# Laying attention output in token order on chip, and storing 128 tokens as one transfer

## The chip, the cores and the metric

The kernel runs on one NeuronCore of one Trainium2 chip. The time is the device time of one execution in microseconds; of several executions the median is given. Five engines work side by side, each through its own list of instructions in order: TensorE (PE), VectorE (DVE), ScalarE (ACT), GpSimd (POOL) and SyncE (SP). PE's loads of stationary weights are shown as PEld. A transfer (DMA) is issued by one of the queues of SP, ACT or POOL, and 16 DMA engines carry it out.

## The reference

Eight batches of attention with twelve heads whose scores are mixed across heads before the softmax and after it, then a two-layer network with a squared relu on each token:

```python
scores = scale * np.matmul(q, k.transpose(0, 1, 3, 2))   # q, k, v: 8 x 12 x 448 x 64
scores = np.einsum('bhij,hg->bgij', scores, w_pre)
attn = np.exp(scores - np.max(scores, axis=-1, keepdims=True))
attn = attn / (np.sum(attn, axis=-1, keepdims=True) + 1e-09)
attn = np.einsum('bhij,hg->bgij', attn, w_post)
x = np.matmul(attn, v)           # to (8 * 448) x (12 * 64) = 3584 x 768
h = np.maximum(x @ w_in, 0.0)    # w_in 768 x 2048
out = h * h @ w_out              # w_out 2048 x 768, out 3584 x 768, float32
```

## The kernel before

**Tokens and chunks.** The 448 tokens of a batch fall into a tail of the last 64 (block r = 0) and three blocks r = 1, 2, 3 of 128: a block holds every third of the first 384 tokens, so that row p of block r is token 3p + r - 1. Scores are made per block (`score`, L718): matmuls into a PSUM bank, copied as bf16 to `snat`, 128 tokens by 12 heads by 448 keys. To mix heads, the kernel needs head and token together in the partitions. `relayout` (L769) does that with one DMA on SP's queue for each chunk of ten tokens (`sch`, 120 rows of ten tokens by twelve heads). 45 such chunks make a batch, 360 the whole kernel.

**Which ten tokens.** In blocks 1 to 3 a relayout takes every twelfth row of the block: o, o + 12, and so on (L798). From batch 1 on (`PAIR_FROM`) two chunks are mixed together (`mix_two`, L824), in quarters of the PE array, and the ten tokens of a result are every sixth row of one half of 120. Rows 120 to 127 of the blocks are gathered in chunks of their own (cc = 0). In batch 0, block 1 and the first chunk of block 2 are "direct" (`is_direct`): they are mixed without a relayout, and their ten tokens stand side by side.

**A chunk** (`chunk`, L850): PE mixes the heads into a bank (L891, L837); VectorE takes the maximum of each row (L902); ScalarE computes the exponential with its sum (L905); VectorE takes reciprocals (L912); GpSimd multiplies the second mixing matrix by them (`wq`, L915); PE mixes heads again and turns the result over at once, four matmuls into a bank of 112 keys by 4 x 12 x 10 (L922); VectorE or ScalarE copies the bank to `atb` as bf16 (`f_ac`, L929, through the helper `copy`, L533 on VectorE and L535 on ScalarE). `places` (L808) says at which columns of `atb` the tokens of the chunk stand: ten next to one another, chunk after chunk. So a column of `atb` is a position and not a token.

**The rest.** `av` (L956) multiplies `atb` with the values (L968) and copies to `xt`; its list of chunks that it needs comes from `touches` (L980). `unit` (L1010) runs the network over 128 or 256 positions: first layer L1027, relu L1041 or L1045, square on GpSimd L1048, second layer L1066, and copies of 128 positions by 384 columns into one of two buffers `osb`. When both halves are there, the stores go out (L1090). Because positions are not tokens, `pieces` (L1101) gives two transfers for 128 positions of a block: 120 rows, whose destination steps through chunks and slots, and 8 rows for the chunks of their own. The 64 positions of a tail are one transfer. Both go through GpSimd's queue, except for the last 128 positions, which go out in three column cuts, the 120 rows on SP's queue and the 8 rows on ACT's.

**Order.** The program's order is written by a planner (class `Planner`, L147 for `run`) before the kernel is built. Every piece of work is an operation with engines that may take it, an assumed duration and a priority; the planner plays time forward and lists, for each engine, what comes next. A copy that VectorE or ScalarE may do goes to whichever comes free first. A chunk's number n is its priority; scores and relayouts of a chunk have n minus `AHEAD` and so come earlier (L737, L777, L797). Network matmuls have a priority behind all chunks and fill what is left of PE. Transfers are modelled with two queues (`moved`, L142): a number of rows, and ns for each row alone and beside the other queue.

The copy and the stores:

```python
for half, x0, s0, w in where:
    copy(
        eng, atb[half][:, :, :, x0:x0 + w].rearrange("p j g m -> p (j g) m"),
        slots[ak][0:P_KEYS, 0:NB * H * ns].rearrange("p (a m) -> p a m", m=ns)[:, :, s0:s0 + w],
    )
```

Of the kernel before, what the change touches and what calls it, by code (L numbers as in the profile page):

```python
# [23 lines left out]
NJ = 3  # L24
# [16 lines left out]
PIECE = NPAIR // 2  # L41
NE = 6
NSCH = 14
AHEAD = 7.7
FIFO = 50
IDLE_NS, IDLE_COLS, IDLE_FROM, IDLE_END, IDLE_LOW = 112, 256, 1300, 130000, 0.62
SPELL, PHASE, DROP, RISE = 3413, 1700, 0.4, 0.8
# [292 lines left out]
def kernel(  # L340
# [370 lines left out]
    def is_direct(b, c):  # L711
        return b == 0 and C0[1] <= c <= C0[2]
# [95 lines left out]
    def places(b, c):  # L808
        r, cc = block_of(c)
        rest, first = (0, NS) if b % 2 else (P_ROWS, 0)  # L810
        if r == 0:
            return [(0, rest + CI * cc, 0, CI)]
        half, base = [(0, first), (1, 0), (1, P_ROWS)][r - 1]
        if cc > 0:
            return [(half, base + CI * (cc - 1), 0, CI)]
        if b == 0 and r > 1:
            return [(0, rest + 62, 0, 2), (1, 120, 2, 8)] if r == 2 else [(1, P_ROWS + 120, 0, 8)]
        return [
            [(0, rest + 60, 0, 2), (0, first + 120, 2, 8)],
            [(0, rest + 62, 0, 2), (1, 120, 2, 6)],  # L820
            [(1, 126, 0, 2), (1, P_ROWS + 120, 2, 8)],
        ][r - 1]

    def mix_two(b, cs):  # L824
# [25 lines left out]
    def chunk(b, c):  # L850
# [76 lines left out]
                )  # L927

        def f_ac(eng):  # L929
            for half, x0, s0, w in where:  # L930
                copy(
                    eng, atb[half][:, :, :, x0:x0 + w].rearrange("p j g m -> p (j g) m"),
                    slots[ak][0:P_KEYS, 0:NB * H * ns].rearrange("p (a m) -> p a m", m=ns)[:, :, s0:s0 + w],
                )

# [20 lines left out]
    def av(b, half, gs, x0, x1):  # L956
        to = [(max(c0, x0), t0 + max(x0 - c0, 0), min(c0 + w, x1) - max(c0, x0)) for c0, t0, w in spans(b % 2, half)]
        to = [span for span in to if span[2] > 0]
        keys = [("g", "v", b, half, g, x0) for g in gs]

        def mms(*got):
            for g, slot in zip(gs, got):
                v_ = slot[:, :].rearrange("p (a c) -> p a c", a=2)
                for i in range(2):
                    c2 = 2 * g + i
                    for jb in range(NB):
                        for hh in range(2):
                            nc.tensor.matmul(  # L968
                                v_[64 * hh:64 * hh + 64, i, 0:x1 - x0],
                                lhsT=vs[:, 2 * c2 + hh, jb, :],  # L970
                                rhs=atb[half][:, jb, 2 * c2 + hh, x0:x1],
                                start=(jb == 0), stop=(jb == NB - 1),
                            )

        def evac(eng, g, key):
            v_ = slots[key][:, :].rearrange("p (a c) -> p a c", a=2)
            for c0, t0, w in to:
                copy(eng, xt[:, 2 * g:2 * g + 2, t0:t0 + w], v_[:, :, c0 - x0:c0 - x0 + w])

        def touches(c):  # L980
            return any(h_ == half and p0 < x1 and p0 + w > x0 for h_, p0, _, w in places(b, c))

        cs = [place_of(b, c) for c in range(NCHUNK) if touches(c)]
        old = []
        if b == 1:
            old += relay_of[0]
        if b >= 2:
            for a, z in units_of(b // 2 - 1):
                if any(a < t0 + w and z > t0 for _, t0, w in to):
                    old += h_op[b // 2 - 1, a]  # L990
        pri = max(cs) + 3
        mm = add(
            "PE", 60 + 48 * (x1 - x0) // 14 * len(gs), pri, keep(keys, mms), [ac_op[n] for n in cs] + v_in[b] + old, lat=200,
            bank=keys, mode=COLS,
        )
        av_op.setdefault((b, half), []).append(mm)
        for g, key in zip(gs, keys):
            xc = add(
                {"ACT": 440, "DVE": 540} if len(to) == 1 else {"ACT": 650, "DVE": 750}, 0, pri,
                lambda eng, g=g, key=key: evac(eng, g, key), [mm], lat=100, frees=key,  # L1000
            )
            for _, t0, w in to:
                xc_op.setdefault(b // 2, []).append((t0, t0 + w, xc))
# [6 lines left out]
    def unit(pair, ui):  # L1010
# [47 lines left out]
        for mt in range(w // 128):  # L1058
            whole = not (z == W2B and mt == 1 and pair == B // 2 - 1)
            cuts = [0, 384, DMODEL] if whole else [0, 384, 640, DMODEL]  # L1060
            for nt, (c0, c1) in enumerate(zip(cuts, cuts[1:])):
                key = ("f", ix, "o", mt, nt)
                for f0 in range(0, FT, OSTEP):
                    def mms(slot, f0=f0, mt=mt, c0=c0, c1=c1):
                        for ft in range(f0, f0 + OSTEP):
                            nc.tensor.matmul(  # L1066
                                slot[:, 0:c1 - c0], lhsT=h2_[:, ft, mt * 128:(mt + 1) * 128],
                                rhs=w2[:, ft, c0:c1],
                                start=(ft == 0), stop=(ft == FT - 1),
                            )  # L1070
                    if f0 == 0:
                        prev = add("PE", (12 + (c1 - c0) * 5 // 3) * OSTEP / 4, fill + 20 + 4 * mt + 2 * nt, keep(key, mms),
                                   [prev] + sq_op[ix][0:max(1, OSTEP // nf)] + w2_in[0:1 if ix < SOON else 4], lat=0, bank=key)
                    else:
                        prev = add("PE", (12 + (c1 - c0) * 5 // 3) * OSTEP / 4, FILL, lambda key=key, mms=mms: mms(slots[key]), [prev, w2_in[f0 // 4]] + sq_op[ix][0:(f0 + OSTEP + nf - 1) // nf], lat=0)
                    o_op[ix].append(prev)
                end = add("WAIT%s" % str(key), 0, 0, lambda: None, [prev], lat=200)
                si = ix_store[0]

                def evac(eng, key=key, si=si, c0=c0, c1=c1):  # L1080
                    copy(eng, osb[si % 2][:, c0:c1], slots[key][:, 0:c1 - c0])

                ev = add({"DVE": 80 + (c1 - c0) * 25 // 24, "ACT": 165 + (c1 - c0) * 5 // 7}, 0, 0, evac, [end, st_op.get(si - 2)] + ([m_op[n_] for n_ in direct] if si < 2 else []), lat=100, frees=key)
                evs = evs + [ev] if nt == 1 and whole else [ev]
                if nt == 1 or not whole:
                    done = []
                    for rows, dst, o in pieces(pair, a + mt * 128, None if whole else (c0, c1)):
                        side_ = not whole and rows <= CI
                        def store(dst=dst, o=o, rows=rows, si=si, e0=0 if whole else c0, e1=DMODEL if whole else c1, eng=nc.scalar if side_ else nc.gpsimd if whole else nc.sync):
                            eng.dma_start(out=dst, in_=osb[si % 2][o:o + rows, e0:e1])  # L1090
                        done.append(add("ACT" if side_ else "POOL" if whole else "SP", 510 if rows <= CI else 830 if whole else 930, FILL, store, evs))
                    for op in done:
                        op.store = whole
                    st_op[si] = pl.moved("LOAD" if whole else "DMA", 64, 31, 31, 0, done, 700)
            if whole:
                ix_store[0] += 1

# [3 lines left out]
    def pieces(pair, pos, part=None):  # L1101
        e0, e1 = (0, DMODEL) if part is None else part
        got = []
        for bb in range(2):
            row = (2 * pair + bb) * S
            for j, first in enumerate(PLACES[bb]):
                o = first + bb * S - pos
                if not 0 <= o < 128:
                    continue
                if j == NJ:  # L1110
                    got.append((NS, out[row + TAIL:row + S, e0:e1], o))
                    continue
                if row == 0 and j == 0:
                    got.append((P, out[0:TAIL, :].rearrange("(p r) e -> p r e", r=NJ)[:, 0, e0:e1], o))
                    continue
                view = out[row:row + CPR * CI * NJ, :].rearrange(
                    "(s c r) e -> r c s e", c=CPR // 2 if 2 * pair + bb >= PAIR_FROM else CPR, r=NJ,
                )
                got.append((CPR * CI, view[j, :, :, e0:e1], o))
                part_ = out[row:row + TAIL, :].rearrange("(p r) e -> p r e", r=NJ)  # L1120
                got.append((8, part_[CPR * CI:P, j, e0:e1], o + CPR * CI))
        return got

    def gate(step):
# [209 lines left out]
```

## Time and profile before

| | |
|---|---|
| median of 3 executions | 573.57 us (572.86 to 578.93) |
| the profiled execution | 574.74 us, span 573.0 us |
| mean granted PE clock | 0.996 of full speed |
| PE / VectorE / ScalarE / GpSimd busy | 560.2 / 495.3 / 451.5 / 378.3 us |
| store issues on GpSimd's queue | 53: 22 of 120 rows, 22 of 8 rows, 8 of 64 rows, 1 of 128 rows |
| atb copies of 112 x 480 | 178 on VectorE, mean 648 ns; 158 on ScalarE, mean 562 ns |
| HBM read, written | 45.61 MB, 11.01 MB |

The span runs from the first to the last instruction of the profiled execution; some 1.7 us lie around it. A line of a group reads: line of the kernel, engine, operation, what is written from what, partitions x elements and type, count, then busy time in us and the mean ns of one, then the time the engine sat idle just before these instructions and what ended it. Lines of the helper `copy` carry L533 or L535 whatever is copied, so the tile's name tells them apart. A "busy" PE need not run at its peak: the time from one matmul's end to the next one's says how fast it goes.

### The profile page before, as it was taken

Reading aid. Unit: us, or ns where it says so; the run is one execution under the profiler, and the core shown is the slowest. Engines: PE = TensorE matmul, PEld = TensorE weight load, DVE = VectorE, ACT = ScalarE, POOL = GpSimd, SP = SyncE. Lnnn points to the kernel's source line nnn. Section 1 sums busy time; section 2 is a strip of 40 time slices with the busy share of each in tenths; the row PEclk is TensorE's granted clock in tenths of the full one; section 3 lists DMA queues with packets and bytes.
Section 4 is the critical chain, followed back from the end, with each engine's and each line's share of the span. In section 5 each row is a group of like instructions: output and inputs, shape, how many; then the busy total and the mean of one; then the engine's idle time right before and its main releaser. Section 6 shows DMA issues by size and latency. Waiting matters only on the chain.

```text
span 573.0 us, 17975 instructions
## 1 busy us (share of the span) xinstructions
PE 560.2 (98%) x6323; PEld 396.6 (69%) x6323; DVE 495.3 (86%) x1101; ACT 451.5 (79%) x1194; POOL 378.3 (66%) x697
## 2 busy tenths in 40 slices
PE   8999999999999899999999999999999999999996
PEld 4767756785676657677677577767667566767784
DVE  7999999999999689998897998988799888988441
ACT  6799999789888688888988888987988888887200
POOL 9867447784795539767687468957598454747451
PEclk9999999999999989999999999999999999999999
DMA  9999849963999529954798649975496745422011
GB/s 134 212 201 220 160 108 213 179 161 97 178 185 143 142 81 180 182 147 103 142 208 139 148 112 162 178 141 142 108 204 153 154 125 100 131 78 79 5 53 56
DMA packets 132505, 80.89 MB, mean 141 GB/s; under 512 B 61748, under 2 KB 129062, under 8 KB 132414
## 3 DMA queue, kind: packets, MB, share of 16 engines
q0 software_dynamic: 51664, 33.45, 37.4%
q1 hardware_dynamic: 80702, 46.26, 34.2%
q8 instruction: 49, 0.80, 0.5%
q14 instruction: 42, 0.34, 0.2%
q10 hardware_dynamic: 48, 0.02, 0.0%
HBM read 45.61 MB, written 11.01 MB: 99 GB/s over the span
## 4 chain that ended last, share of the span: by engine, by line
PE 89%; DVE 5%; DMA 2%; ACT 2%; issue 1%; POOL 1%; DVEq 0%; POOLq 0%; ACTq 0%
PE bank L1066 26%; PE bank L1027 25%; PE bank L922 14%; PE bank L732 7%; PE bank L968 7%; PE bank L837 5%; PE bank L891 3%; DVE mn L902 2%; DMA sch<-snat 1%; ACT es L905 1%; PE bank L897 1%; DVE osb L880 1%; DMA qs<-in_q_dram 1%; DVE atb L533 1%; DVE snat L533 1%
## 5 line engine op out<-in xcount | busy, mean ns | idle before, releaser
L905 ACT ACTIVATE es<-bank,mn 124x448 bf16<-124x448 f32 (+1 forms) x360 | 228.4, 642 | 36.9 <-DVE mn L902 32.3
L902 DVE TENSOR_REDUCE mn<-bank 124x1 f32<-124x448 f32 (+1 forms) x360 | 208.9, 611 | 3.2 <-PE bank L837 2.5
L1066 PE MATMUL bank<-w,h 128*128 128x384 bf16 (+2 forms) x912 | 179.0, 324 | 0.5 <-DVE osb L533 0.4
L1027 PE MATMUL bank<-xt,w 128*128 128x256 bf16 (+1 forms) x1632 | 164.2, 254 | 0.4
L1027 PEld LDWEIGHTS <-w 128*128 128x128 bf16 x1632 | 133.0, 98 | 26.6 <-issue 13.5
L1048 POOL TENSOR_TENSOR h<-hr 128x512 bf16<-128x512 f32 x112 | 116.0, 1038 | 32.1 <-DVE hr L1041 14.3
L915 POOL TENSOR_SCALAR wq<-wback_two,rc 124x120 bf16<-124x120 f32 x252 | 88.8, 363 | 71.8 <-DVE rc L912 52.0
L533 DVE CAST atb<-bank 112x480 bf16<-112x480 f32 (+1 forms) x201 | 122.2, 618 | 10.9 <-PE bank L922 10.1
L922 PEld LDWEIGHTS <-es 124*112 124x112 bf16 (+2 forms) x1440 | 107.1, 130 | 28.2 <-issue 5.8
L1066 PEld LDWEIGHTS <-h 128*128 128x128 bf16 x912 | 80.3, 98 | 58.4 <-issue 18.0
L922 PE MATMUL bank<-wq,es 124*112 124x120 bf16 (+2 forms) x1440 | 118.8, 218 | 1.2 <-ACT es L905 0.4
L535 ACT CAST atb<-bank 112x480 bf16<-112x480 f32 (+3 forms) x182 | 95.5, 536 | 17.0 <-PE bank L922 16.1
L535 ACT CAST snat<-bank 128x448 bf16<-128x448 f32 x177 | 89.6, 546 | 10.4 <-PE bank L732 5.5
L533 DVE CAST snat<-bank 128x448 bf16<-128x448 f32 x141 | 83.1, 611 | 6.6 <-DMA sch<-snat 4.2
L905 ACT ACTIVATION_READ_ACCUMULATOR es<-bank,mn 124x1 f32 (+1 forms) x360 | 75.0, 208 | 0.0
L1041 DVE TENSOR_SCALAR hr<-bank 128x512 f32<-128x512 f32 x74 | 50.9, 688 | 20.4 <-PE bank L1027 17.0
L915 POOL TENSOR_SCALAR wq<-wback,rc 124x120 bf16<-124x120 f32 (+1 forms) x94 | 33.5, 365 | 43.5 <-DVE rc L912 32.1
L1090 POOL DMA_DIRECT2D out_dram<-osb x53 | 33.2, 627 | 29.9 <-DVE osb L533 17.5
L732 PE MATMUL bank<-kt,qz 64*64 64x448 bf16 (+1 forms) x528 | 47.6, 365 | 2.5 <-DVE snat L533 2.5
L837 PE MATMUL bank<-sch,wmix 64*64 64x448 bf16 x504 | 42.3, 362 | 0.0
L968 PE MATMUL bank<-atb,vs 112*64 112x192 bf16 (+3 forms) x864 | 40.6, 250 | 0.0
L968 PEld LDWEIGHTS <-vs 112*64 112x64 bf16 x864 | 36.6, 110 | 4.6 <-issue 4.2
(80 smaller groups left out, 398.7 us busy)
## 6 DMA issues: line engine op xcount, KB each, us to landing
sch<-snat SPq DMA_DIRECT2D x318, 105.0 KB
out_dram<-osb POOLq DMA_DIRECT2D x22, 360.0 KB, 6.1
vs<-in_v_dram POOLq DMA_DIRECT2D x16, 336.0 KB, 7.6
ks<-in_k_dram POOLq DMA_DIRECT2D x14, 336.0 KB, 8.7
qs<-in_q_dram POOLq DMA_DIRECT2D x14, 288.0 KB, 7.9
w<-in_moe_w_in_dram POOLq DMA_DIRECT2D x6, 512.0 KB, 13.7
w<-in_moe_w_out_dram POOLq DMA_DIRECT2D x4, 768.0 KB, 20.7
out_dram<-osb POOLq DMA_DIRECT2D x8, 192.0 KB, 5.3
```

The lines of the kernel that those rows point to most:

```text
L533: nc.vector.tensor_copy(out=out_, in_=in_)
L535: nc.scalar.copy(out=out_, in_=in_)
L732: nc.tensor.matmul(slot[m0:m1, 0:S], lhsT=lhsT[:, m0:m1], rhs=kt[i][half, :, at_, :], start=True, stop=True,)
L837: nc.tensor.matmul(got[i + x][o0:o1, 0:S], lhsT=w[k0:k1, c0:c0 + o1 - o0], rhs=srcs[i + y][k0:k1, :], start=True, stop=True,)
L902: nc.vector.tensor_reduce(out=mn[i][0:rows, :], in_=slots[mk][0:rows, 0:S], axis=AX.X, op=ALU.min)
L905: nc.scalar.activation(out=es[i][0:rows, 0:S], in_=slots[mk][0:rows, 0:S], func=ACT.Exp, scale=-1.0, bias=mn[i][0:rows, 0:1], accum_out=sm ...
L915: nc.gpsimd.tensor_scalar(out=wq[i][0:rows, :, 0:ns], in0=back[0:rows, :, 0:ns], scalar1=rc[i // 2][0:rows, i % 2:i % 2 + 1], scalar2=1.0, ...
L922: nc.tensor.matmul(slot[0:P_KEYS, jb * H * ns:(jb + 1) * H * ns], lhsT=es[i][0:rows, jb * P_KEYS:(jb + 1) * P_KEYS], rhs=wq[i][0:rows, :, ...
L968: nc.tensor.matmul(v_[64 * hh:64 * hh + 64, i, 0:x1 - x0], lhsT=vs[:, 2 * c2 + hh, jb, :], rhs=atb[half][:, jb, 2 * c2 + hh, x0:x1], start ...
L1027: nc.tensor.matmul(slot[:, j * w:(j + 1) * w], lhsT=w1[c2][:, (f0 + j) * 128:(f0 + j + 1) * 128], rhs=xt[:, c2, a:z], start=(c2 == 0), sto ...
L1048: nc.gpsimd.tensor_tensor(out=h2_[:, f0:f0 + nf, 0:w], in0=hr[gi % 2][:, :].rearrange("p (f c) -> p f c", f=nf), in1=hr[gi % 2][:, :].rear ...
L1066: nc.tensor.matmul(slot[:, 0:c1 - c0], lhsT=h2_[:, ft, mt * 128:(mt + 1) * 128], rhs=w2[:, ft, c0:c1], start=(ft == 0), stop=(ft == FT - 1),)
```

## The change

A chunk's ten tokens are now written into `atb` where their block's rows belong: at every sixth column from batch 1 on, at every twelfth in batch 0, and side by side for direct chunks. `places` gives a step with each place, `f_ac` writes with that step, and `touches` counts a place from its first to its last column. A column of `atb` is then a row of the block, and `pieces` gives one transfer of 128 rows (destination every third token). `AHEAD` goes from 7.7 to 8.0, and the planner's assumed ns for each of a store's 64 rows from 31 to 16.

```diff
-AHEAD = 7.7
+AHEAD = 8.0
...
         rest, first = (0, NS) if b % 2 else (P_ROWS, 0)
         if r == 0:
-            return [(0, rest + CI * cc, 0, CI)]
+            return [(0, rest + CI * cc, 0, CI, 1)]
         half, base = [(0, first), (1, 0), (1, P_ROWS)][r - 1]
         if cc > 0:
-            return [(half, base + CI * (cc - 1), 0, CI)]
+            o = cc - 1
+            if is_direct(b, c):
+                return [(half, base + CI * o, 0, CI, 1)]
+            if b >= PAIR_FROM:
+                return [(half, base + o // 2 + CPR * CI // 2 * (o % 2), 0, CI, CPR // 2)]
+            return [(half, base + o, 0, CI, CPR)]
...
-            for half, x0, s0, w in where:
+            for half, x0, s0, w, step in where:
                 copy(
-                    eng, atb[half][:, :, :, x0:x0 + w].rearrange("p j g m -> p (j g) m"),
+                    eng, atb[half][:, :, :, x0:x0 + step * (w - 1) + 1:step].rearrange("p j g m -> p (j g) m"),
...
-            return any(h_ == half and p0 < x1 and p0 + w > x0 for h_, p0, _, w in places(b, c))
+            return any(h_ == half and p0 < x1 and p0 + st * (w - 1) + 1 > x0 for h_, p0, _, w, st in places(b, c))
...
-                    st_op[si] = pl.moved("LOAD" if whole else "DMA", 64, 31, 31, 0, done, 700)
+                    st_op[si] = pl.moved("LOAD" if whole else "DMA", 64, 16, 16, 0, done, 700)
...
-                if row == 0 and j == 0:
-                    got.append((P, out[0:TAIL, :].rearrange("(p r) e -> p r e", r=NJ)[:, 0, e0:e1], o))
-                    continue
-                view = out[row:row + CPR * CI * NJ, :].rearrange(
-                    "(s c r) e -> r c s e", c=CPR // 2 if 2 * pair + bb >= PAIR_FROM else CPR, r=NJ,
-                )
-                got.append((CPR * CI, view[j, :, :, e0:e1], o))
-                part_ = out[row:row + TAIL, :].rearrange("(p r) e -> p r e", r=NJ)
-                got.append((8, part_[CPR * CI:P, j, e0:e1], o + CPR * CI))
+                got.append((P, out[row:row + TAIL, :].rearrange("(p r) e -> p r e", r=NJ)[:, j, e0:e1], o))
```

The places of the chunks of rows 120 to 127 are as before, with a step of 1.

More of the change, by code (lines that the diff above doesn't have):

```diff
@@ L811, in places @@
         if r == 0:
-            return [(0, rest + CI * cc, 0, CI)]
+            return [(0, rest + CI * cc, 0, CI, 1)]
         half, base = [(0, first), (1, 0), (1, P_ROWS)][r - 1]
         if cc > 0:
-            return [(half, base + CI * (cc - 1), 0, CI)]
+            o = cc - 1
[4 more added lines that the diff above has]
+            return [(half, base + o, 0, CI, CPR)]
         if b == 0 and r > 1:
-            return [(0, rest + 62, 0, 2), (1, 120, 2, 8)] if r == 2 else [(1, P_ROWS + 120, 0, 8)]
+            return [(0, rest + 62, 0, 2, 1), (1, 120, 2, 8, 1)] if r == 2 else [(1, P_ROWS + 120, 0, 8, 1)]
         return [
-            [(0, rest + 60, 0, 2), (0, first + 120, 2, 8)],
-            [(0, rest + 62, 0, 2), (1, 120, 2, 6)],
-            [(1, 126, 0, 2), (1, P_ROWS + 120, 2, 8)],
+            [(0, rest + 60, 0, 2, 1), (0, first + 120, 2, 8, 1)],
+            [(0, rest + 62, 0, 2, 1), (1, 120, 2, 6, 1)],
+            [(1, 126, 0, 2, 1), (1, P_ROWS + 120, 2, 8, 1)],
         ][r - 1]
```

## The prediction

> **What bounds the kernel now.** I read the share of each engine first, then the chain that ended last, then engine time by stretch, then the waits of the one full engine.
>
> ```profile
> span 573.0 us, 17975 instructions
> ...
> PE 560.2 (98%) x6323; PEld 396.6 (69%) x6323; DVE 495.3 (86%) x1101; ACT 451.5 (79%) x1194; POOL 378.3 (66%) x697
> ...
> PE 89%; DVE 5%; DMA 2%; ACT 2%; issue 1%; POOL 1%; DVEq 0%; POOLq 0%; ACTq 0%
> ```
>
> TensorE is busy in 98% of the span and is 89% of the chain. GpSimd, whose store issues the change cuts, is busy in 66%. By stretch (columns: the stretch, its length, busy us of PE, weight loads, DVE, ACT, POOL, clock, DMA share, GB/s):
>
> ```profile
> 40.00:80.00 40.00, 38.94 (x585) 28.30 (x586) 38.63 (x90) 36.91 (x102) 21.18 (x41) 1.00 0.94 176
> ...
> 200.00:500.00 300.00, 297.82 (x3317) 209.60 (x3317) 269.90 (x582) 255.90 (x675) 205.80 (x380) 0.99 0.72 145
> ```
>
> From 200 to 500 us PE idles 2.2 us of 300, VectorE 30.1, ScalarE 44.1, GpSimd 94. From 40 to 80 us VectorE is as full as PE: it idles 1.4 us of 40. The waits (total us, times, longest) say who holds whom:
>
> ```profile
> POOL wq L915 <- DVE rc L912: 88.7, 62, 3.8
> POOL out_dram L1090 <- DVE osb L533: 17.5, 4, 7.6
> PE bank L732 <- DVE snat L533: 2.5, 2, 2.2
> PE bank L922 <- POOL wq L915: 0.3, 1, 0.3
> ```
>
> GpSimd waits 88.7 us for the softmax sums. PE waits for GpSimd 0.3 us. So time can fall only by what PE does less of, by its few stalls, or at the two ends; it can rise if VectorE or ScalarE runs out of slack.
>
> **Stores taken away.** The group of store issues:
>
> ```profile
> L1090 POOL DMA_DIRECT2D out_dram<-osb x53 | 33.2, 627 | 29.9 <-DVE osb L533 17.5
> ```
>
> 53 issues on GpSimd become 31 (23 of 128 rows, 8 of 64): all 22 of 8 rows go. Those stand second in their pair at 0.53 to 0.58 us each, so GpSimd saves 22 x 0.55 = 12 us. It lies beside PE's work: GpSimd idles 94 us of 300 and PE's wait for it is 0.3 us. I take 0, at best -1 us. The wait for the osb copy stays, with one issue instead of two behind it, so the wq queued behind it starts 0.5 us sooner. The three 8-row issues on ACT's queue go as well; ScalarE has no other work by then.
>
> **The end.** The last matmul ends at 568.2 us, the last osb copy at 568.6, SP issues the last store from 568.66, its last packet ends at 571.5, the span at 573.0. The queues in the last 7 us:
>
> ```profile
> q1 hardware_dynamic: 378, 0.37, 17.1%
> ```
>
> SP's three stores are 3 x 120 rows = 360 packets of data; the other 18 are of 4 bytes, 6 per store: completion marks of six engines. The row before the last packet is thus 20 rows deep on each of six. The last store took 1.4 us from about 570.1 (its issue plus the 1.45 us from first issue to first packet) to 571.5. The new one is 128 rows; spread over 16 engines it is 8 deep, 8/20 x 1.4 = 0.6 us: -0.8 us. Bounds 0 (engines not the limit) and -1.0; I take -0.7. [...]
>
> **TensorE's order.** The planner writes all orders anew. Counting crossings between full-array matmuls and those that use part of it (L732, L837, L968) in the two programs' orders: 330 before, 318 after, with the same 6323 matmuls. By the end times in the trace a 64*64 448-column matmul ends 180 ns after its like but 303 after a full-array one (+123); a 384-column full-array one 163 ns after its like, 269 after a 64*64 one (+106). Six pairs less: 6 x 0.229 = -1.4 us.
>
> **AHEAD 8.0.** Score and relayout priorities move up by 0.3 chunk, about 0.5 us (360 chunks in 573 us). No instruction is added: SP still issues the same relayouts and transposes. PE's longest stall (2.2 us at 201 us, L732) began with snat copies that waited 3.0 us for a relayout to leave their buffer; 9 us before, two stores had been issued and landed after 8 us. Shortly after, the granted clock was 0.5 for 3.4 us (213.5 to 216.9), worth 1.7 us. Both could go; equally, the new order can have its own. I take 0, bounds -3.9 and +4 (one more such pair). The planner also shifts copies: VectorE gets 12 snat and 3 relu more, 5 atb and 7 osb less: 12 x 0.611 + 3 x 0.688 - 5 x 0.648 - 7 x 0.551 = +2.3 us, ScalarE about -2.2. Beside their idle time: 0.
>
> **Strided atb copies.** This is the cost. Of 336 copies of 480 elements, 252 (134 on VectorE, 118 on ScalarE) now write bf16 every 12 bytes, and 24 (13 and 11, all of batch 0) every 24 bytes; 60 stay contiguous. Counts, tiles and matmuls are otherwise the same, and so is the number of waits per engine: no copy waits for another because its columns now interleave. No row shows a strided write. Nearest rows (us busy, mean ns):
>
> ```profile
> L533 DVE CAST atb<-bank 112x480 bf16<-112x480 f32 x178 | 114.5, 648 | 10.7 <-PE bank L922 9.9 <-ACT snat L535 0.2
> ...
> L533 DVE CAST atb<-bank 112x96 bf16<-112x96 f32 x11 | 2.7, 248 | 0.2 <-PE bank L922 0.2
> ...
> L533 DVE CAST xt<-bank 128x128 bf16<-128x128 f32 x6 | 1.7, 281 | 0.0
> ...
> L479 DVE TENSOR_REDUCE smask_far<-ident 120x10 f32<-120x120 bf16 x1 | 0.4, 371 | 0.0
> L465 DVE TENSOR_REDUCE own<-ident 124x12 f32<-124x120 bf16 x1 | 0.4, 355 | 0.0
> ...
> L482 DVE TENSOR_REDUCE far<-ident 120x12 f32<-120x120 bf16 x1 | 0.3, 267 | 0.0
> ```
>
> Low end: the 96-element copies write runs of 2 with a jump after each. At 1.04 ns per element, 128 elements in 281 ns make 248 for 96: measured 248, so the jumps are free. ScalarE's are 247 against 275 - 32 x 0.83 = 248. High end: reads in steps of 20 and 24 bytes (L479, L465) take 104 and 88 ns more than the same 120 elements in sequence (L482): 0.73 to 0.87 ns each, 0.35 to 0.42 us for 480. For 12 bytes I take 0: the write row is the nearest, a write against a read. For 24 bytes, where every write jumps, the read price: 13 x 0.38 = 5 us on VectorE where it idles about 1.4 us per 40; on PE between 0 and +3.6, taken +1.0, since half of VectorE's copies there are not what PE waits for next.
>
> **Sum.** -1.4 - 0.7 + 1.0 = -1.1 us on the profiled execution, 574.74 us (span 573.0 and 1.74 around it): 573.6. The median, 573.57, is 1.17 us lower, so **572.5 us**. Own range with the bounds above: 568 to 577.
>
> **Rivals.**
> *Strided writes cost at 12 bytes too (slower).* Place: the 134 VectorE copies. Between 200 and 500 us there are 134 x 300/460 = 87 of them against 30.1 us idle, so VectorE is the bound from +0.35 us each: the read price. Half of it (+0.19) fills 17 of the 30 us; VectorE is then 96% busy as in 40 to 80 us, where PE idles 1.06 of 40 against 0.29 per 40 later: 0.77/40 of 460 us is +9; with +0 as its low end, about +5: 578. At the full price 87 x 0.39 = 34 us exceed the idle time by 4, and all slack between the engines is gone: +9 and +6 more, 588. Against: the free runs of two. Chance 0.27. [...]
> *The stall at 201 us and the half-clock spell both go (faster).* -2.2 - 1.7 with the terms above, 24-byte copies free, on the median: 573.6 - 1.4 - 0.7 - 3.9 = 567.6. For: stores land sooner and relayouts start earlier. Against: the order is new everywhere. Chance 0.18.
> *The new order stalls more.* One more stall and spell on top of the forecast, 572.5 + 3.9 = 576.4. For: VectorE has no slack from 40 to 80 us. Against: from 200 to 500 us PE met one such pair. Chance 0.10.
> *The change does not do what it says:* ruled out by the counts of issues and patterns in the built program.
> My forecast: 0.45.
>
> **Numbers.** About 1% is what a measurement of this kernel can tell from no change: 567.8 and 579.3 are the lines. Faster: half of the second rival (its 567.6 stands on the line), 0.09, and 0.04 of the forecast: 0.13. Slower: the part of the first rival above half the read price, 0.16, with 0.03 each of the third and of the forecast: 0.22. Same: the rest, 0.65. The range takes in the forecast, the 578 and half of the way on to 588, and below it the second rival with 1.6 us for a lower clock loss elsewhere: 566 to 583; about 0.1 stays above and 0.06 below.
>
> **What will show it.** The mean of the 112x480 atb copies on both engines (648 and 562 ns now): within 20 ns, my low end is right; +0.2 or more, the first rival. The 24-byte ones between 45 and 85 us, near 1.0 us. 31 store issues on GpSimd, near 20 us busy. Last packet 0.7 us nearer to the last matmul. The L732 stall and the half-clock spell, gone or not. The forecast falls if strided copies are dear, or if PE's idle time and clock differ by more than 4 us.

## The result, and the profile after

The changed kernel takes 717.53 us (median, 715.47 to 717.86) against 573.57: 1.248 times as long, interval 1.241 to 1.254. The forecast was 572.5, in a range of 566 to 583. The page of the changed kernel, with the lines that answer to those shown before:

```profile
span 715.8 us, 17922 instructions
...
PE 618.7 (86%) x6323; PEld 416.2 (58%) x6323; DVE 641.1 (90%) x1102; ACT 591.5 (83%) x1193; POOL 363.7 (51%) x675
...
PE 18%; DVE 14%; ACT 11%; issue 5%; DMA 3%; POOL 1%; ACTq 0%; DVEq 0%; SPq 0%; POOLq 0%
```

PE has as many matmuls as before and is no longer the full engine. VectorE is busy for 146 us more, ScalarE for 140, and the time grew by 144. The two stretches looked at before (stretch, length, busy us of PE, weight loads, VectorE, ScalarE, GpSimd, clock, DMA share, GB/s):

```profile
40.00:80.00 40.00, 31.82 (x458) 23.69 (x458) 35.20 (x66) 35.15 (x67) 14.88 (x29) 0.83 0.94 164
200.00:500.00 300.00, 259.13 (x2636) 172.90 (x2629) 278.11 (x452) 266.74 (x538) 159.75 (x302) 0.98 0.59 122
```

From 200 to 500 us PE idles 41 us of 300, where it idled 2.2. VectorE idles 22. What was added is one kind of instruction, in the groups by shape (count, busy us, mean ns, idle before):

```profile
L533 DVE CAST atb<-bank 112x480 bf16<-112x480 f32 x173 | 282.2, 1663 | 10.2 <-PE bank L927 9.4 <-ACT xt L535 0.2 <-ACT snat L535 0.2
...
L535 ACT CAST atb<-bank 112x480 bf16<-112x480 f32 x163 | 255.9, 1595 | 16.2 <-PE bank L927 15.4
```

The mean, 648 and 562 ns before, still mixes contiguous and strided copies. The order of the built program tells which copy has which step and first column; with the trace's durations this gives (median ns, VectorE / ScalarE; a line is an aligned stretch of 16 bytes of a partition, by which the durations go here and, for lone bf16 elements, in the first table of copies below):

| step of the write | 16-byte lines under ten elements | VectorE | ScalarE |
|---|---|---|---|
| 2 bytes (in sequence) | 2 | 648 | 563 |
| 12 bytes | 7 | 1640 | 1662 |
| 12 bytes | 8 | 1855 | 1876 |
| 24 bytes | 10 | 2253 | 2297 |

The two engines take nearly the same time although their copies in sequence differ, and a copy beside a strided one of the other engine is no slower: on VectorE the copies over eight lines take 1878 ns in the mean where none runs beside them (14 copies) and 1881 where one does throughout (4). So VectorE pays this without the other's doing, and it is no quarrel between the two.

Not all of a strided copy's recorded time is lost to its engine. The next instruction's record begins 299 ns before the strided copy's record ends on VectorE and 405 ns on ScalarE (medians); behind other instructions it is 80 and 111. So the busy time of the two engines grew by less than the sum of the copies did. Against the run with contiguous writes below (497.2 and 449.7 us busy) it is 286 us over 276 strided copies, 1.04 us for each, where the recorded durations grew by 335.

PE now waits for these copies, for a bank or for the chunk behind it (waits of the changed kernel: total us, times, longest; the first line is GpSimd's):

```profile
POOL wq L920 <- DVE rc L917: 184.5, 94, 7.6
...
PE bank L927 <- DVE atb L533: 8.8, 14, 1.1
```

GpSimd's wait for the softmax sums doubled from 88.7 us: chunks arrive late, so everything behind them does. That the columns of a chunk are now spread out adds no wait of its own: `av` reads whole blocks of columns (0 to 128, 128 to 192 or 256, 0 to 192, 0 to 256), so `touches` names the same chunks as before.

The stores did what was forecast. The group of GpSimd's issues in the changed kernel:

```profile
L1095 POOL DMA_DIRECT2D out_dram<-osb x31 | 18.5, 598 | 32.5 <-DVE osb L533 19.8 <-ACT osb L535 8.1 <-DVE rc L917 2.4
```

SP's issues of the last three (shortest, median and longest ns, first and last start):

```profile
L1095 SPq DMA_DIRECT2D out_dram<-osb x3: 332/344/391, 710.6 to 712.9; - x3
```

SP's queue in the last 7 us (packets, MB, share of 16 engines):

```profile
q1 hardware_dynamic: 432, 0.39, 16.6%
```

GpSimd has 31 issues in 18.5 us; its 128-row stores land 3.7 us after their issue in the median. SP's three last stores are 3 x 128 = 384 rows and 48 marks of 4 bytes, 16 per store in place of 6. From the last matmul to the end of the span it is 3.2 us, 4.7 before.

### The profile page after: what moved, and what is told of

Its sections match the earlier page's. It is cut to its first block, busy times and chain, and to the rows that moved or that the text cites. A ratio compares the mean times of both kernels' runs of the same rounds, so it can differ in the third digit from the quotient of the medians.

```text
span 715.8 us, 17922 instructions
## 1 busy us (share of the span) xinstructions
PE 618.7 (86%) x6323; PEld 416.2 (58%) x6323; DVE 641.1 (90%) x1102; ACT 591.5 (83%) x1193; POOL 363.7 (51%) x675
## 4 chain that ended last, share of the span: by engine, by line
PE 18%; DVE 14%; ACT 11%; issue 5%; DMA 3%; POOL 1%; ACTq 0%; DVEq 0%; SPq 0%; POOLq 0%
DVE atb L533 7%; PE bank L1032 6%; PE bank L1071 6%; ACT atb L535 5%; ACT es L910 4%; DVE mn L907 4%; DMA sch<-snat 2%; PE bank L973 2%; PE bank L927 2%; DVE snat L533 1%; ACT snat L535 1%; PE bank L732 1%; PE bank L842 1%; DMA out_dram<-osb 1%; DVE rc L917 1%
## 5 line engine op out<-in xcount | busy, mean ns | idle before, releaser
L533 DVE CAST atb<-bank 112x480 bf16<-112x480 f32 (+1 forms) x194 | 289.5, 1526 | 11.9 <-PE bank L927 11.1
L535 ACT CAST atb<-bank 112x480 bf16<-112x480 f32 (+3 forms) x189 | 263.3, 1431 | 17.5 <-PE bank L927 16.7
L910 ACT ACTIVATE es<-bank,mn 124x448 bf16<-124x448 f32 (+1 forms) x360 | 237.6, 672 | 48.6 <-DVE mn L907 37.1
L1071 PE MATMUL bank<-w,h 128*128 128x384 bf16 (+2 forms) x912 | 185.1, 327 | 2.5 <-DVE atb L533 1.6
L927 PE MATMUL bank<-wq,es 124*112 124x120 bf16 (+2 forms) x1440 | 126.7, 220 | 22.3 <-DVE atb L533 8.8
L533 DVE CAST snat<-bank 128x448 bf16<-128x448 f32 x153 | 94.3, 633 | 3.3 <-PE bank L732 1.9
L732 PE MATMUL bank<-kt,qz 64*64 64x448 bf16 (+1 forms) x528 | 59.8, 369 | 14.0 <-DVE atb L533 5.1
L842 PE MATMUL bank<-sch,wmix 64*64 64x448 bf16 x504 | 55.1, 364 | 16.5 <-DVE atb L533 5.2
L917 DVE RECIPROCAL rc<-sm 124x2 f32<-124x2 f32 (+1 forms) x180 | 34.0, 189 | 20.1 <-ACT es L910 16.2
L732 PEld LDWEIGHTS <-qz 64*64 64x64 bf16 (+1 forms) x528 | 19.1, 104 | 44.4 <-issue 39.8
```

The lines of the kernel that those rows point to most:

```text
L533: nc.vector.tensor_copy(out=out_, in_=in_)
L535: nc.scalar.copy(out=out_, in_=in_)
L732: nc.tensor.matmul(slot[m0:m1, 0:S], lhsT=lhsT[:, m0:m1], rhs=kt[i][half, :, at_, :], start=True, stop=True,)
L842: nc.tensor.matmul(got[i + x][o0:o1, 0:S], lhsT=w[k0:k1, c0:c0 + o1 - o0], rhs=srcs[i + y][k0:k1, :], start=True, stop=True,)
L910: nc.scalar.activation(out=es[i][0:rows, 0:S], in_=slots[mk][0:rows, 0:S], func=ACT.Exp, scale=-1.0, bias=mn[i][0:rows, 0:1], accum_out=sm ...
L927: nc.tensor.matmul(slot[0:P_KEYS, jb * H * ns:(jb + 1) * H * ns], lhsT=es[i][0:rows, jb * P_KEYS:(jb + 1) * P_KEYS], rhs=wq[i][0:rows, :, ...
```

## The experiments

**Each part alone.** Strided writes taken back, everything else of the change left:

```diff
-            return [(half, base + o, 0, CI, CPR)]      # and its sixth-column form
+            return [(half, base + CI * (cc - 1), 0, CI)]   # places, f_ac, touches as before
...
```

> The changed kernel with one part undone: the ten tokens of a chunk are written side by side into atb again, as in the kernel before; the 128-row stores, AHEAD 8.0 and the planner's 16 ns per row stay. The 120 rows of each block therefore land in another order in the output, which this kernel leaves wrong. Theory (the strided writes alone make the loss): 112x480 atb copies back at 648 ns on VectorE and 562 on ScalarE, time 568 to 577 us, the forecast of 572.5 among them. Rival (the single store or the new order cost much by themselves): over 585 us.

Measured 571.69 us, ratio to the kernel before 0.9966 (0.9937 to 0.9995). Its page:

```profile
span 569.9 us, 17922 instructions
...
PE 559.2 (98%) x6323; PEld 396.7 (70%) x6323; DVE 497.2 (87%) x1102; ACT 449.7 (79%) x1193; POOL 364.7 (64%) x675
...
L533 DVE CAST atb<-bank 112x480 bf16<-112x480 f32 (+1 forms) x194 | 118.6, 623 | 8.6 <-PE bank L922 7.7
...
L535 ACT CAST atb<-bank 112x480 bf16<-112x480 f32 (+3 forms) x189 | 99.2, 539 | 18.9 <-PE bank L922 17.3
```

PE is full again. The other half, strided writes put into the kernel before and nothing else (`places`, `f_ac` and `touches` of the change; the stores, AHEAD 7.7 and 31 ns as before):

```diff
...
-                    eng, atb[half][:, :, :, x0:x0 + w].rearrange(...)
+                    eng, atb[half][:, :, :, x0:x0 + step * (w - 1) + 1:step].rearrange(...)
```

> The kernel before with one part of the change alone: atb is written at every sixth (batch 0: twelfth) column, while the 120-row and 8-row stores, AHEAD 7.7 and 31 ns stay as before. The output rows of each block land in another order, which this kernel leaves wrong. Theory (the strided writes alone make the loss): 276 copies of 1.6 to 2.3 us, VectorE near 640 us busy, time 710 to 725 us. Rival (stores and order share in it): under 690 us.

Measured 715.04 us, ratio 1.250 (1.245 to 1.255). The two runs together show that the writes make the whole loss, and that the rest of the change, beside contiguous writes, is a gain of 0.3%, with an interval that just leaves out none.

**AHEAD.** The kernel before with one constant changed:

```diff
-AHEAD = 7.7
+AHEAD = 8.0
```

> The kernel before with AHEAD 8.0 alone. It shows what a redrawn order is worth by itself. Theory (an order redrawn by the planner moves this kernel by a few us at most): 570 to 578 us. Rival (7.7 is a sharp optimum and 8.0 costs several per cent): over 585 us.

Measured 579.86 us, ratio 1.015 (1.009 to 1.020): between the two expectations, and more than my "few us". The same 8.0 with single stores (the first run) is 0.3% faster than before. So a redrawn order can cost several us, and the constant has no worth of its own here. Whether an order alone can gain as much no run shows.

**What a strided write costs.** Copies of one bank appended behind the end of the kernel before, one form per line:

```diff
+        for x in range(3):
+            nc.vector.tensor_copy(out=flat[:, :, 0:10], in_=src)          # L1312, 48 runs of ten in sequence
+            nc.vector.tensor_copy(out=flat[:, :, 1:11], in_=src)          # L1313, from an odd element
+            nc.vector.tensor_copy(out=flat[:, :, 0:19:2], in_=src)        # L1314, then steps 3, 4, 6 (L1317)
...
+            nc.vector.tensor_copy(out=flat[:, :, 4:59:6], in_=src)        # L1318, step 6 over eight lines
+            nc.vector.tensor_copy(out=flat[:, :, 0:73:8], in_=src)        # L1319; L1320 step 12
+            nc.vector.tensor_copy(out=..., in_=...)                       # L1321, runs of two every 24 bytes
+            nc.vector.tensor_copy(out=f32v[:, :, 0:10], in_=...)          # L1322 float32, then steps 3 and 6
...
+            nc.vector.tensor_copy(out=line[:, 0:480], in_=plain)          # L1325; L1326 reads the bank turned
...
```

> The kernel before, with copies of one PSUM bank appended behind its end: each line of the appended block is one form of copy, three times on VectorE, then three times on ScalarE. Theory A (each 16-byte line that a copy touches with separated elements costs 4.3 ns, from 7 lines 1641 ns, 8 lines 1855, 10 lines 2253, fixed part about 200): for 48 runs of ten bf16, steps of 2, 3, 4, 6, 8, 12 elements touch 3, 4, 5, 7, 10, 10 lines and take 0.8, 1.0, 1.2, 1.65, 2.25, 2.25 us; runs of two with a jump of 24 bytes 1.2 us; float32 in steps of 12 and 24 bytes (120 elements) 0.5 and 0.7 us against 0.27 in sequence; a run of ten that starts on an odd element 0.65. Rival B (a lone 2-byte write costs, whatever line it is in, since it fills half of a 4-byte word): step 2 already about 1.6 us or more, all steps alike; runs of two as fast as ten in sequence, 0.65 us; float32 at any step 0.27; odd start about 1.0. For the table of reads: a strided read of 12 bytes from SBUF and a turned read of PSUM, written in sequence, somewhere from 0.55 to 1.1 us.

Groups by shape in that part of the trace (VectorE's, mean ns behind the comma):

```profile
L1319 DVE CAST atb<-bank 112x480 bf16<-112x480 f32 x3 | 6.8, 2270 | 0.1
L1320 DVE CAST atb<-bank 112x480 bf16<-112x480 f32 x3 | 6.7, 2239 | 0.1
...
L1317 DVE CAST atb<-bank 112x480 bf16<-112x480 f32 x3 | 4.9, 1631 | 0.1
L1316 DVE CAST atb<-bank 112x480 bf16<-112x480 f32 x3 | 3.7, 1225 | 0.1
...
L1315 DVE CAST atb<-bank 112x480 bf16<-112x480 f32 x3 | 3.0, 993 | 0.1
...
L1314 DVE CAST atb<-bank 112x480 bf16<-112x480 f32 x3 | 2.4, 801 | 0.1
...
L1313 DVE CAST atb<-bank 112x480 bf16<-112x480 f32 x3 | 2.0, 663 | 0.1
L1326 DVE CAST atb<-bank 112x480 bf16<-112x480 f32 x3 | 2.0, 658 | 0.1
L1321 DVE CAST atb<-bank 112x480 bf16<-112x480 f32 x3 | 2.0, 658 | 0.1
L1312 DVE CAST atb<-bank 112x480 bf16<-112x480 f32 x3 | 2.0, 656 | 0.1
...
L1324 DVE COPY osb<-bank 112x120 f32<-112x120 f32 x3 | 1.1, 372 | 0.1
...
L1323 DVE COPY osb<-bank 112x120 f32<-112x120 f32 x3 | 1.0, 319 | 0.1
...
L1322 DVE COPY osb<-bank 112x120 f32<-112x120 f32 x3 | 0.8, 272 | 0.0
```

Neither expectation came out whole. For lone bf16 elements the count of lines was right for every step: 3, 4, 5, 7, 10 and 10 lines gave 801, 993, 1225, 1631, 2270 and 2239 ns. It failed where whole 4-byte words are written: runs of two 658 ns instead of 1.2 us, float32 at 24 bytes 372 instead of 700. The rival failed at small steps (801 at step 2, not 1.6 us) and at the odd start (663, not 1.0 us). ScalarE's strided rows are the same within 5 ns except at eight lines (L1318: 1944 on VectorE, 2033 on ScalarE). That row starts otherwise than the others. It writes columns that the copy ahead doesn't, so it does not wait for that one, and its record begins before the other's ends (start and length in us):

```profile
577.84 1.63 DVE L1317 CAST atb<-bank 112x480 bf16<-112x480 f32 x1
579.20 1.94 DVE L1318 CAST atb<-bank 112x480 bf16<-112x480 f32 x1
```

From the end of the copy ahead to its own end it is 1680 ns on either engine. The copies that wait for the one ahead start 31 to 35 ns after its end. One more row of the table is a read of SBUF every 12 bytes, written in sequence: 476 ns on VectorE and 826 on ScalarE. Joined, the two expectations give, as an estimate from these rows: a line that gets half a word costs about 4.3 ns ((1631 - 801) / (48 x 4)), one that gets whole words about 1.9 (float32 at 24 bytes: (372 - 147) / 120, with 272 - 120 x 1.04 = 147 as the fixed part, and 1.04 ns per element from copies of 128 and 256 elements in 281 and 414 ns in the kernel before), and either hides behind the time of the elements themselves when a line has enough of them. A second table put that to the test:

```diff
+            nc.vector.tensor_copy(out=...[:, :, :, 0:2], in_=...)   # L1312 runs of two, every 24 bytes
+            nc.vector.tensor_copy(out=...[:, :, :, 1:3], in_=...)   # L1313 the same from an odd element
+            nc.vector.tensor_copy(out=...[:, :, :, 0:2], in_=...)   # L1314 every 16 bytes
+            nc.vector.tensor_copy(out=...[:, :, :, 1:3], in_=...)   # L1315 from an odd element
+            nc.vector.tensor_copy(out=flat[:, 0:24, 0:109:12], in_=src[:, 0:24, :])   # L1316; L1317 step 6; L1318 reads the bank turned
...
```

> The kernel before with a second table of copies behind its end, three times on VectorE, then on ScalarE, 480 elements unless told. Theory (a 16-byte line that gets a write of half a 4-byte word costs about 4.3 ns, a line that gets whole words alone about 1.9 ns, and either hides under 1.04 ns per element; fixed part 150 to 200 ns): runs of two from an even element every 24 bytes 0.65 us, every 16 bytes 0.65; the same from an odd element, each run thus in halves of two words: every 24 bytes (five or six lines per ten) 1.2 to 1.45 us, every 16 bytes (five lines) 1.2; 240 elements at 24 bytes 1.2 us, at 12 bytes 0.9. Rival (what counts is whether the next element is a neighbour, not whole words): runs of two from an odd element as fast as from an even one, 0.65.

Groups by shape of that run:

```profile
L1316 DVE CAST atb<-bank 112x240 bf16<-112x240 f32 x3 | 3.7, 1236 | 0.0
L1315 DVE CAST atb<-bank 112x480 bf16<-112x480 f32 x3 | 3.7, 1226 | 0.1
...
L1313 DVE CAST atb<-bank 112x480 bf16<-112x480 f32 x3 | 3.6, 1199 | 0.1
L1317 DVE CAST atb<-bank 112x240 bf16<-112x240 f32 x3 | 2.7, 896 | 0.1
...
L1314 DVE CAST atb<-bank 112x480 bf16<-112x480 f32 x3 | 2.0, 658 | 0.1
L1312 DVE CAST atb<-bank 112x480 bf16<-112x480 f32 x3 | 1.9, 644 | 0.0
```

Runs of two from an even element take 644 and 658 ns, no more than ten in sequence (656); the same runs from an odd element, each now two halves of words, take 1199 and 1226. The rival is out. Why half a word costs more no run shows.

**Does idle time take it up?** The forecast's first rival let VectorE's idle time swallow up to 0.35 us per copy. One block of three strided, then two:

```diff
-            if is_direct(b, c):
+            if is_direct(b, c) or r < 3:      # two blocks: r < 2
```

> The changed kernel with strided writes in one of three blocks alone (r = 3): 84 copies at 12 bytes and 12 at 24, the other 180 written side by side, so their rows land in another order in the output, which this kernel leaves wrong. They add 84 x 1.2 + 12 x 1.7 = 121 us over two engines that idle 78 and 122 us in the kernel before. Theory A (slack takes it first, then the engines are the bound): 575 to 592 us. Rival B (each strided copy costs the same whether or not there is slack): 572 + 144 x 96/276 = 622 us.

> The same with two of three blocks strided (r = 2 and 3): 168 copies at 12 bytes and 24 at 24, 242 us more over the two engines, against 200 us of idle time in the kernel before; rows of block 1 land in another order, which this kernel leaves wrong. Theory A (slack first): 610 to 650 us. Rival B (linear): 572 + 144 x 192/276 = 672 us.

Measured 625.92 us, ratio 1.086 (1.080 to 1.092), and 681.2, ratio 1.182 (1.174 to 1.191): linear, the expectation of slack falls. But whole blocks are a full dose in places. So the same copies spread: every third, then every sixth pair of chunks.

```diff
-            if is_direct(b, c):
+            if b == 0 or (o // 2) % 3:        # every sixth: b == 0 or o // 2
```

> The changed kernel with strided writes in every third pair of chunks, in all three blocks from batch 1 on (4 of 12 chunks of a block), the rest side by side; their rows land in another order in the output, which this kernel leaves wrong. 84 copies at 12 bytes add 84 x 1.2 = 101 us, 50 on each engine, as the run with one strided block, but spread. Theory A (time follows the added work, since the idle time of VectorE and ScalarE is waiting inside each chunk's chain and can't be used): 0.446 us of time for each us of added copy, as with one block: 572 + 45 = 617 us. Rival B (with the dose spread, idle time of 78 and 122 us takes it up): 574 to 592.

> The same with every sixth pair strided (2 of 12 chunks of a block): 42 copies at 12 bytes, 50 us in all, 25 on each engine. Rows of the others land in another order, which this kernel leaves wrong. Theory A (time follows the added work): 572 + 22 = 594 us. Rival B (idle time takes it up): 572 to 578. If this run shows nothing and the one with every third pair shows its share, there is a threshold between 25 and 50 us on each engine.

Measured 619.24 us, ratio 1.078 (1.073 to 1.083), and 588.72, ratio 1.024 (1.019 to 1.030). Against the run with contiguous writes (571.69 us; 118.6 + 99.2 us of atb copies; 497.2 and 449.7 us busy), with the sums over both engines:

| strided copies | recorded copy time added, us | busy time added, us | time added, us | time per us of copies | time per us busy |
|---|---|---|---|---|---|
| every sixth pair | 47.1 | 35.5 | 17.0 | 0.36 | 0.48 |
| every third pair | 100.0 | 83.8 | 47.6 | 0.48 | 0.57 |
| one block | 117.8 | 102.2 | 54.2 | 0.46 | 0.53 |
| two blocks | 235.4 | 201.8 | 109.5 | 0.47 | 0.54 |
| all (the change) | 335.0 | 285.7 | 145.8 | 0.44 | 0.51 |

Half of the added time falls on each of two engines, so 0.5 means that no idle time is used. The busy time is the measure for it, since part of a strided copy's record lies over the next instruction. By it no dose uses idle time to speak of: the 0.48 of the smallest is not told apart from 0.5 when a redrawn order can cost several us, and above 0.5 a little is lost besides. One stretch shows it, block 3 of batch 3 and the first chunks behind it, cut to the same instructions but for one or two (columns as in the stretches above). In the run with stores only, contiguous:

```profile
253.00:280.00 27.00, 26.97 (x290) 19.77 (x289) 24.43 (x54) 23.51 (x65) 16.17 (x30) 1.00 0.39 117
```

In the run with one block strided:

```profile
277.00:311.00 34.00, 30.54 (x291) 20.55 (x291) 30.48 (x55) 30.72 (x66) 16.26 (x31) 1.00 0.33 101
```

7.0 us longer, for 6.1 us more on VectorE and 7.2 on ScalarE. VectorE idles 2.6 us in the first and 3.5 in the second, ScalarE 3.5 and 3.3: the idle time stays, PE's idle time appears.

**Was it the planner?** It assumed 565 and 600 ns for copies that take three times as long. Told otherwise:

```diff
+        {"DVE": 1720, "ACT": 1760} if where[0][4] > 1 else
         {"DVE": 565 * len(where), "ACT": 600 * len(where)} if len(where) == 1 else ...
```

> The changed kernel whole, with one number of the planner corrected: a strided atb copy is assumed to take 1720 ns on VectorE and 1760 on ScalarE instead of 565 and 600. The work is the same, its order and its share between the two engines are not. Theory A (most of the loss is an order written for copies of a third of their length): the two engines' busy time of 641 + 592 us, levelled, is 616 each, and with the ends the time falls to 640 to 670 us. Rival B (the two engines' capacity and the chain through each chunk set the time, whatever the order): 700 to 720 us.

Measured 714.95 us, ratio 1.241 (1.231 to 1.251): rival B. Its page:

```profile
PE 635.4 (89%) x6375; PEld 440.9 (62%) x6375; DVE 636.0 (89%) x1113; ACT 603.5 (84%) x1182; POOL 362.9 (51%) x675
...
PEclk9999999799699959999799967999989985999979
```

PE has 52 fillers more and was granted half its clock for 126 us of this run, 31 in the changed kernel, so a better order could hide behind a slower PE. It does not: from 90 to 680 us, 62 atb copies of 480 elements begin in the 117 us at half clock (0.53 per us) and 233 in the 473 us at full clock (0.49), and in the changed kernel's full clock it is 0.51. Chunks pass no faster where PE is at full clock, so PE's pace is not the bound there. Why the last tenth of VectorE and sixth of ScalarE can't be filled (the chain from maximum to exponential to sum to wq to the copy crosses both for each chunk) is only argued: one other order was tried, and it fills them no better.

**The aim without the price.** The table has a read of PSUM turned, in steps of 80 bytes, at 658 ns (ScalarE 558), beside 643 and 607 for a plain one. The plain one did not wait for the copy ahead and the turned one did. Where the turned one doesn't wait, in the second table (L1318 and L1326), its record has 747 and 750 ns; from end to end it is 483 and 398, as the plain one's 487 and 399. So turning costs nothing, and token order can be made in the copy from the bank of attention times values to `xt`, which moves an eighth of the elements per partition of the atb copies:

```diff
-                copy(eng, xt[:, 2 * g:2 * g + 2, t0:t0 + w], v_[:, :, c0 - x0:c0 - x0 + w])
...
+                        copy(
+                            eng, o_[:, :, 0:CPR * CI].rearrange("p a (u k) -> p a u k", k=k_),
+                            i_[:, :, 0:CPR * CI].rearrange("p a (k u) -> p a u k", k=k_),
+                        )
+                        copy(eng, o_[:, :, CPR * CI:P], i_[:, :, CPR * CI:P])   # rows 120 to 127
...
```

with `places` as before, the change's `pieces` and 16 ns, 700 and 800 ns assumed for these copies, and either AHEAD.

> A repair: atb is written side by side as before; token order is made one step later, in the copy from the bank of attention times values to xt, which reads the bank turned (120 positions as 6 x 20 or 12 x 10) and writes in sequence, with a small copy for the 8 rows left. Stores are the 128-row ones of the change; AHEAD 7.7. The table of copies has the turned read at 658 ns on VectorE and 558 on ScalarE, as fast as a plain one. Added: about 3 copies more per group of two head pairs and batch, some 0.5 us, 24 groups: 12 to 15 us over two engines with 200 us idle. Theory (the change's aim is worth what the run with stores alone gave, about -2 us, and the small copies hide): 568 to 575 us. Rival (small copies sit in front of the network's first layer and show): 576 to 585.

> The same repair with AHEAD 8.0, the order of the change. AHEAD 8.0 alone made the kernel before 1.5% slower, and with the single stores it was 0.3% faster: theory (which order comes out is worth some us either way, and no property of 8.0): 568 to 580 us, and it cannot be told beforehand which of the two is faster. Rival (8.0 suits the single stores): 3 us or more faster than with 7.7.

Measured 573.19 us, ratio 0.9969 (0.9943 to 0.9995), and 572.71, ratio 0.9959 (0.9929 to 0.9989), beside 575.3 us for the kernel before on the same chip. Both are faster than both kernels, by 2 to 3 us (0.3 to 0.4%) against the one before, with intervals that just leave out none; between them nothing can be told. The copies to `xt`:

```profile
L535 ACT CAST xt<-bank x95: 178/303/552, 19.4 to 541.2; 128x240 bf16<-128x240 f32 x39, 128x16 bf16<-128x16 f32 x39, 128x128 bf16<-128x128 f32 x12, 128x448 bf16<-128x448 f32 x4
L533 DVE CAST xt<-bank x76: 160/281/615, 16.0 to 539.6; 128x240 bf16<-128x240 f32 x30, 128x16 bf16<-128x16 f32 x30, 128x128 bf16<-128x128 f32 x12, 128x448 bf16<-128x448 f32 x2
```

They became 171, from 69 before; the turned ones of 240 elements take 398 ns on VectorE and 377 on ScalarE, plain ones of 256 in the run with stores only 419 and 381. VectorE and ScalarE are as busy as in the kernel before (498.7 and 452.7 us with AHEAD 7.7).

## Why the prediction was wrong, step by step

**The strided copies: the step that failed.** "For 12 bytes I take 0: the write row is the nearest, a write against a read." Measured: +0.99 to +1.21 us on VectorE and +1.1 to +1.3 on ScalarE, and +1.6 to +1.7 at 24 bytes, where 0.38 was taken. The free row of runs of two was read as "jumps are free". Those rows held something equal that the change did not: their runs were whole 4-byte words (in the second table such runs take 644 ns, and 1199 from an odd element). The high end failed too. 0.42 us came from reads, and a lone 2-byte write costs 4.3 ns per line where those reads cost 0.7 to 0.9 ns more per element. A bound from an operation of another kind is no bound. The durations count by lines of 16 bytes: 1640, 1855 and 2253 ns on VectorE for 7, 8 and 10 of them. Four elements in a line don't yet give full speed: at step 2 a full line gets four bf16 elements, and the copy still takes 801 ns against 656.

**The rival that pointed this way** had the place right and the price wrong by three to six times, and its decision point was wrong in kind. That half of the read price might be paid (+0.19 us per copy, which gave 578) no run shows: in the changed kernel the strided copies take 0.99 us or more over those in sequence on both engines. The rival let idle time absorb up to 0.35 us per copy; the dose runs show that time follows added work from the start, at 0.48 to 0.57 us for each us that the two engines are busy longer.

**PE bounds the kernel:** true of the kernel before and of the run with stores only (busy in 98% of the span in both), and it is why the other terms were small.

**Stores:** right. 31 issues, 18.5 us, GpSimd 13.6 us less busy in the run with stores only, where 12 us was forecast, and none of it that could be told apart in the time.

**The end:** right in direction, under-sized. From the last matmul to the end went from 4.74 to 3.18 us in the run with stores only, -1.6 where I took -0.7 and bounded at -1.0. That 128 rows spread over 16 engines was my estimate, which no view of the kernel before had shown. In the changed kernel each of SP's last stores has 16 marks in place of 6, and from 713.1 to 713.4 us its queue's packets take 100% of 16 engines' time, where they took 30.7% from 570.1 to 571.5 us before. Besides, SP's issue itself became shorter, 734 to 343 ns, which I had not looked for.

**Order:** -1.4 us of crossings can't be told apart in the total. The bound of +4 was too narrow: AHEAD 8.0 alone cost 5 us in the medians (579.86 against 574.56 beside it) and 1.5% in the ratio. The half-clock spell was put at 213.5 us by a time that was not counted from the span's start; it lies at 202.8 to 206.2, behind the stall that ends at 201. In the run with stores only that stall and that spell are gone (PE waits for snat 0.5 us at most, and the clock is 1.00 from 200 to 500 us), but its mean clock is 0.996 as before.

**The sum of all but the strided copies** was -2.1 us, 571.5; the run with stores only has 571.69. That they meet is partly luck: the end gave -1.6 and not -0.7, and beside the kernel before on its own chip (574.56) the run is 2.9 us faster.

## What to carry to other kernels

Before a copy's write pattern is changed, ask whether it still fills whole 4-byte words: a bf16 copy of 480 elements whose last dimension has a step of 2 to 12 took 801 to 2270 ns here on either engine, where ten in sequence took 656 on VectorE and 560 on ScalarE. Put the turn on the PSUM read side, where it cost nothing here (483 ns against 487 on VectorE, 398 against 399 on ScalarE), or into a copy that moves fewer elements. And do not count an engine's idle tenth as room in a kernel whose chunks pass through it several times: measure with a part of the dose (here 0.48 to 0.57 us for each us that two engines are busy longer, from the smallest on), and by the engines' busy time rather than by the sum of recorded durations.

## What the runs showed of the hardware that I had not expected

- A bf16 copy from PSUM of 480 elements with lone 2-byte writes costs by the 16-byte lines under it, some 4.3 ns each, and the same on VectorE and ScalarE (L1317 1631 ns, ScalarE's 1631), though in sequence they differ (656 and 560).
- Runs of two elements: 644 ns from an even element, 1199 from an odd one.
- A read of PSUM in steps of 80 bytes with a write in sequence costs nothing on either engine (from end to end 483 against 487 ns on VectorE, 398 against 399 on ScalarE).
- In the changed kernel an instruction's record begins before that of the one ahead on its engine ends: behind a strided copy by 299 ns on VectorE and 405 on ScalarE in the median, behind others by 80 and 111. So recorded durations can't be added up as an engine's time.
- One store of 128 rows is issued by SP in 343 ns, one of 6 x 20 rows in 734 ns; on GpSimd's queue the 128-row stores land in 3.7 us in the median in the changed kernel, the 120-row ones in 6.1 in the kernel before. Over all stores the median is 5.8 us before, 4.0 in the run with stores only and 3.8 in the changed kernel.
